# Cluster assignment of an attention and soft-MoE kernel: scores folded by a matmul, one argmax per head pair, and a new order table

## The chip, the cores and the metric

The kernel runs on one core of a Trainium2 chip, as one launch. The metric is the device time of the launch in microseconds (us), lower is better. TensorE (PE in the rows, PEld its weight loads) multiplies, VectorE (DVE), ScalarE (ACT) and GpSimd (POOL) do the elementwise work and the reductions, SyncE (SP) only issues transfers.

## The reference

Three layers in a row, all in fp32. Cut to what matters here:

```python
# 1. attention inside clusters: 2 batches, 8 heads, 768 tokens, 64 dims, 16 centroids per head
q_assign = argmax(q_n @ c_n.T, -1); k_assign = argmax(k_n @ c_n.T, -1)   # rows normalised
scores = where(q_assign[:, None] == k_assign[None, :], q @ k.T / 8, -1e9)
attn = softmax(scores); x = (attn @ v)            # -> 1536 tokens x 512
# 2. soft MoE: 8 experts x 4 slots, hidden 1024
logits = x @ phi; d = softmax(logits, axis=0); slot_in = d.T @ x
slot_out[e] = relu(slot_in[e] @ w1[e]) @ w2[e]; x = softmax(logits, axis=1) @ slot_out
# 3. gated MLP: xn = rms_norm(x) * g; out = (silu(xn @ w_gate) * (xn @ w_val)) @ w_out
```

## The kernel before

**Work of the attention.** The 16 heads are taken in 8 pairs (`prepare(i)`), and each pair in two units (`unit(u)`, u = 0 to 15), which are halves of 384 queries. `prepare` loads k, q, v, splits k and q into a high and a low part (`split_hi`, `split_lo`), transposes them (`trans`, `evac`), and for each half g of 384 tokens finds the cluster: `cluster` multiplies k and q with the centroids (the centroids' high and low parts give two partial scores for each cluster), `cevac` copies the result to the tile cs, `clusterT` transposes it by three matmuls with the identity, `part` adds the two partial scores on DVE, `argmax(0..4)` makes a one-hot row on DVE, `onehot` transposes that by three matmuls, and `oq`, `ok` write it on ACT into the tiles q2 and k2 as extra rows, so that the score matmuls mask by themselves. A unit runs six `s1` steps (two matmuls each) with `s1max` on DVE (a maximum over 768 columns), puts the maxima into q2 by `nmT`, `nrow` and the transfer `mrow`, and then runs `s2` (four matmuls), `exp` on ACT, `acc` (sum of the exponentials) on POOL or DVE, and `av` (product with v), six chunks each. It ends with `osb`, the row sums (`lT`; in unit 15 `sums`), the logits (`lgt`, `lgm`, `lga`; in unit 15 `lgx`) and `oT`, `xrow`.

**PSUM.** `ms` is one bank for all small results (cluster scores, the transposed scores and one-hots, `nmT`, `oT`), `big` three double banks, `av` one bank. A step that allocates `ms` waits until every reader of the last owner is done.

**The layers behind.** On DVE and ACT the attention also carries `decode`, which unpacks the weights of layer 3 (tiles da and wgv). `Tail.middle` does the softmax over tokens and the slots (`SITz`), `experts` streams w1 and w2 from HBM, `gates` forms the small matrices of layer 3 and runs its products (`mm`, `silu`, `hf`, `hh`, `hl`, `om`). `warm` steps are bf16 matmuls of the identity with no use of the result.

**What sets the order.** No engine's program is written by hand. Each step goes to `Sched.op` with a cost per engine and a key (its place in the loop plus an offset by step name from the table `KO`). `Sched.run` takes again and again the step that can start first by these costs, with penalties for steps far ahead of the smallest key, and writes it to its engine. So engines that a step may choose from, and the order on each, come out of the costs, the keys and the constants at the head of the file.

Of the kernel before, what the change touches and what calls it, by code (L numbers as in the profile page):

```python
# [75 lines left out]
LP = 29661.17
AP = 30323.71
GP = 23437.43
XP = 14193.79
# [5 lines left out]
    "argmax": -7.66, "oevac": 15.28, "clusterT": 4.46, "lsum": 18.79, "onehot": -17.16, "acc": -43.2, "av": 64.39,
    "evac": 5.39, "bits": -14.11, "nmT": -27.66, "split_lo": -113.15, "s1max": -11.37, "cevac": -22.81, "nrow": 27.7,
    "cluster": 3.33, "csum": -9.29, "lga": -29.9, "lgm": 53.33, "hh": -53.74, "pre": -21.81, "rms0": -0.9, "h2e": 1.32,
    "part": 19.55, "low": 34.12, "soh": 0.05, "hl": -64.4, "gh": 33.13, "cTe": 9.36, "raw": -14.6, "om": 2.67,
    "cT": -27.78, "sot": -2.04, "lo": 15.35, "gcols": -1.89, "put4": -20.61, "x2s": -1.21, "gp": -3.84, "hi": -13.21,
    "silu": -45.95, "x2": -2.94, "rows": 0.57, "siT": -22.16, "si": -125.5, "dz": 42.07, "mx": 82.62, "mp": 13.33,  # L90
    "dexp": 42.88, "sie": 77.66, "cq": -150.62, "qhi": -37.28, "fexp": 13.02, "gram": -5.42, "socs": 55.02,
    "fold": -5.42, "fsi": -40.68, "fz": 36.93, "qlo": -12.45, "drec": 107.19, "mv": -24.49, "linv": 3.64,
    "xrow": -36.25, "exp": 5.99, "trans": -4.27, "mrow": -111.75, "oq": -72.72, "sums": -65.34, "tok": 8.0,
    "ok": -23.12, "centroids_": 77.19, "cols": 10.87, "csm": -5.47, "ds": -5.05, "dsum": -43.94, "fes": -95.7,
    "four": -35.1, "h1": 30.24, "h2": -10.32, "hT": -3.25, "hTe": -15.51, "hf": -20.81, "high": -60.21, "lgt": -76.92,
    "lgx": -146.73, "lgx0": -3.44, "load": 75.86, "mb": 43.64, "mm": 2.44, "mp1": -72.84, "mpT": 21.92, "od": -23.79,
    "oe": 10.8, "put": 18.97, "relu": -53.54, "rms": 5.79, "root": 18.92, "s2": -1.04, "scale": -12.89, "sel": 28.05,
    "setup": -92.11, "siT0": -14.47, "siTe": -23.07, "side": 117.72, "siz": 10.14, "square": -6.93, "to_out": -29.07,
    "to_tail": 8.19, "to_wp": -25.03, "to_wv": -64.29, "to_wx": 38.05, "to_wz": -23.48, "warm": 89.5, "wload": 21.74,
# [1801 lines left out]
```

## Time and profile before

| | |
|---|---|
| median of 3 runs | 494.79 us (494.28 to 495.96) |
| the profiled execution | 493.6 us, of which 491.9 us from its first to its last instruction |

Stretches of the profiled execution, us from its first instruction:

| stretch | us | PE busy | DVE busy | ACT busy | PE clock | GB/s |
|---|---|---|---|---|---|---|
| to the first s2 of unit 0 | 33.9 | 25.25 | 25.30 | 18.54 | 0.92 | 158 |
| to the first s2 of unit 2 | 26.1 | 25.09 | 18.73 | 17.94 | 0.97 | 128 |
| to the first s2 of unit 14 | 200.5 | 187.79 | 179.94 | 146.81 | 0.99 | 132 |
| to the last logits | 31.7 | 31.12 | 12.88 | 16.49 | 0.94 | 259 |
| middle and experts, to their last product | 56.9 | 52.36 | 10.57 | 12.43 | 0.95 | 374 |
| to the first om of layer 3 | 20.3 | 17.91 | 9.04 | 8.98 | 0.83 | 41 |
| layer 3 | 117.5 | 117.00 | 65.25 | 56.83 | 1.00 | 47 |
| last transfer | 5.0 | 0.05 | 0.00 | 1.17 | 0.77 | 172 |

PE clock is the granted share of 2.4 GHz. A matmul's end is modelled, so that PE busy holds some overlap. A releaser in square brackets (`[0.97 <-DVE E L445]`) is what ended the idle time in front of an instruction.

### The profile page before, as it was taken

The numbers are of one execution on the slowest core, as the hardware profiler recorded it, in microseconds if no ns is written. First come the engines' busy times: TensorE is split into PE (matmuls) and PEld (weight loads), VectorE is DVE, ScalarE is ACT, GpSimd is POOL, SyncE is SP. The second block draws the span as 40 slices with busy tenths as digits, with TensorE's granted clock in tenths as the row PEclk, the third lists the DMA queues.
The fourth block names the chain that finished last, engine by engine and source line by source line (L and its number), as shares of the span: only waits on it lengthen the run. The fifth ranks groups of instructions, "written<-read, shape, count | busy, mean of one in ns | idle before, by whom it ended". The sixth has DMA issues, their size and how long they took to land. (4 is left out here: it accounts for less than half of the span.)

```text
span 491.9 us, 7819 instructions
## 1 busy us (share of the span) xinstructions
PE 456.6 (93%) x2794; PEld 330.3 (67%) x2794; DVE 321.7 (65%) x640; ACT 279.2 (57%) x582; POOL 216.5 (44%) x149
## 2 busy tenths in 40 slices
PE   6889998999999999899889998989989999999995
PEld 5766775777768756667667673335528878888884
DVE  6776889799999899788996143021157894444440
ACT  5568585876877866887756602231066664334332
POOL 2319767674877859484738800012025660000000
PEclk9889998999999999999999978999889999999999
DMA  6455415523634345746236949999502402002002
GB/s 173 117 154 171 115 41 151 135 65 97 198 112 150 94 134 171 200 155 190 98 121 227 339 170 362 378 398 392 225 0 90 168 1 87 0 1 85 0 1 85
DMA packets 30822, 71.96 MB, mean 146 GB/s; under 512 B 4064, under 2 KB 10304, under 8 KB 30784
## 3 DMA queue, kind: packets, MB, share of 16 engines
q1 hardware_dynamic: 26080, 55.73, 34.3%
q10 hardware_dynamic: 4704, 15.73, 10.1%
q8 instruction: 22, 0.36, 0.3%
q14 instruction: 16, 0.13, 0.1%
HBM read 61.97 MB, written 3.15 MB: 132 GB/s over the span
## 5 line engine op out<-in xcount | busy, mean ns | idle before, releaser
L242 POOL TENSOR_TENSOR acc<-acc,P 128x768 f32<-128x768 f32 x62 | 119.3, 1925 | 13.9 <-ACT P L587 10.5
L538 DVE TENSOR_REDUCE nm<-s 128x1 f32<-128x768 f32 x96 | 87.3, 948 | 12.5 <-PE s L526 12.0
L587 ACT ACTIVATE P<-s 128x768 f32<-128x768 f32 x96 | 75.3, 812 | 35.3 <-PE s L580 29.5
L1692 PE MATMUL o<-W,hh 128*128 128x512 f32 x288 | 89.9, 393 | 0.1
L578 PE MATMUL s<-q,k 128*128 128x384 f32 x192 | 70.0, 364 | 2.6 <-DVE nm L538 1.3
L604 PE MATMUL o<-P,rawv 128*64 128x384 f32 x384 | 67.8, 494 | 0.0
L580 PE MATMUL s<-q,k 97*128 97x384 f32 x192 | 65.7, 342 | 0.0
L1692 PEld LDWEIGHTS o<-W,hh 128*128 128x128 f32 x288 | 54.1, 188 | 12.5 <-POOL W L242 0.5
L526 PE MATMUL s<-k,q 96*128 96x384 f32 x192 | 52.4, 369 | 5.3 <-DVE nm L538 4.3
L1692 PE MATMUL o<-W,hl 128*128 128x512 f32 x144 | 56.6, 393 | 0.4 <-DVE hl L242 0.4
L242 POOL TENSOR_TENSOR acc<-P,P 128x768 f32<-128x768 f32 x16 | 30.0, 1875 | 46.3 <-ACT P L587 46.3
L578 PEld LDWEIGHTS s<-q,k 128*128 128x128 f32 x192 | 37.2, 194 | 11.4 <-DVE nm L538 3.4
L604 PEld LDWEIGHTS o<-P,rawv 128*64 128x64 f32 x384 | 25.3, 136 | 28.7 <-issue 27.2
L1664 DVE TENSOR_TENSOR hf<-v,sg 128x512 f32<-128x512 f32 x36 | 24.7, 689 | 28.6 <-ACT sg L1660 27.6
L526 PEld LDWEIGHTS s<-k,q 96*128 96x128 f32 x192 | 31.2, 190 | 16.1 <-DVE nm L538 9.9
L580 PEld LDWEIGHTS s<-q,k 97*128 97x128 f32 x192 | 37.2, 194 | 0.0
L1660 ACT ACTIVATE sg<-g 128x512 f32<-128x512 f32 x36 | 21.4, 597 | 27.7 <-PE g L1652 27.5
L234 ACT CAST hh<-hf 128x512 fp32r<-128x512 f32 x36 | 22.3, 621 | 21.9 <-DVE hf L1664 17.8
L242 DVE TENSOR_TENSOR hl<-hf,hh 128x512 fp32r<-128x512 f32 x29 | 21.2, 731 | 17.0 <-ACT hh L234 16.0
L1692 PEld LDWEIGHTS o<-W,hl 128*128 128x128 f32 x144 | 27.0, 188 | 6.9 <-DVE hl L242 0.8
L242 POOL TENSOR_TENSOR tokk<-rawk,tokk 128x384 fp32r<-128x384 f32 x15 | 16.4, 1092 | 33.3 <-DVE tokk L236 17.6
L676 ACT ACTIVATE pl<-pl 128x128 f32<-128x128 f32 x90 | 23.6, 262 | 7.8 <-PE pl L644 4.0
(261 smaller groups left out, 760.1 us busy)
## 6 DMA issues: line engine op xcount, KB each, us to landing
w<-in_moe_w_dram SPq DMA_DIRECT2D x56, 512.0 KB
gate<-in_moe_w_gate_dram ACTq DMA_DIRECT2D x12, 512.0 KB
val<-in_moe_w_val_dram ACTq DMA_DIRECT2D x12, 512.0 KB
out<-in_moe_w_out_dram SPq DMA_DIRECT2D x10, 512.0 KB
rawk<-in_k_dram SPq DMA_DIRECT2D x8, 384.0 KB
rawq<-in_q_dram SPq DMA_DIRECT2D x8, 384.0 KB
rawv<-in_v_dram SPq DMA_DIRECT2D x8, 384.0 KB
k<-k SPq DMA_DIRECT2D x16, 192.0 KB
```

The lines of the kernel that those rows point to most:

```text
L234: nc.scalar.copy(out, in_)
L242: (nc.vector if e == "dve" else nc.gpsimd).tensor_tensor(out, a, b, op=op)
L526: nc.tensor.matmul(ps[:, g, :HQ], T[q2][0:96, h, qb : qb + 128], T[f"k2_{i}_{g}"][0:96, h, :], start=True, stop=True,)
L538: nc.vector.tensor_reduce(T[f"nm{u}"][:, n : n + 1], T[f"s1_{u}{h}{j}"][:, :, :HQ], op=ALU.max, axis=AX.XY, negate=True)
L578: nc.tensor.matmul(ps[:, h, :HQ], T[f"k1_{i}_{g}"][:, h, kb], T[q1][:, h, :], start=True, stop=False)
L580: nc.tensor.matmul(ps[:, h, :HQ], T[f"k2_{i}_{g}"][0:97, h, kb], T[q2][0:97, h, :], start=False, stop=True)
L587: nc.scalar.activation(p, T[f"s2_{u}_{c}"][:, :, :HQ], AF.Exp, scale=float(1.0 / D**0.5))
L604: nc.tensor.matmul(T[f"o{u}"][64 * h : 64 * h + 64, :HQ], T[f"rawv{i}"][:, h, c, :], T[f"P{u}_{c}"][:, h, :], start=(c == 0), stop=(c == N ...
L676: nc.scalar.activation(p, p, AF.Copy, accum_out=ls_()[:, h, j : j + 1])
L1660: nc.scalar.activation(self.tile(f"sg{tg}_{f}", [128, 512], F32, "sg", "outp", 2), T[f"g{tg}_{f}"], AF.Silu)
L1664: nc.vector.tensor_tensor(self.tile(f"hf{tg}_{f}", [128, 512], F32, "hf", "outp", 2), T[f"v{tg}_{f}"], T[f"sg{tg}_{f}"], op=ALU.mult)
L1692: nc.tensor.matmul(T[f"o{tg}{q}"], T[f"{x}{tg}_{f}"][:, ts], T[f"W{f // 6}"][:, w, f % 6, :], start=(f == 0 and n == 0), stop=(f == 11 and ...
```

## The change

1. **Scores.** Each half still has `cluster` and `cevac`, but cs is now one tile for both halves, in the ring P. `clusterT` multiplies cs by a constant `fold` (128 x 64, made once on DVE), which transposes and adds the two partial scores at once, so `part` is gone.
2. **Argmax.** A new function `both` runs `clusterT`, `argmax`, `onehot`, `oq`, `ok` once per pair for 24 groups of scores, where two halves had 12 each. For pair 0 the work of half 1 no longer has tiles of its own, and one of two `warm` steps goes.
3. **Table.** For pair 0 a one-element exponential follows the two `cevac`, so that ACT loads its exponential table there.
4. **First maxima.** `nmT` of unit 0 uses the bank `av`.
5. **End of the attention.** Unit 15's `sums` write 64 equal columns where they wrote one; the second `sums` comes behind the last `av`, where it was ahead of it; all its `acc` are on DVE.
6. **Behind it.** The row sum of the second softmax (`csm(3)`) waits for the slots; `cols` writes each of its results eight times (64 columns for 8); more `warm` matmuls, eight of them new, ahead of `gram`.
7. **Order.** New constants and a new table `KO`.

```diff
-SH = 6.48
-WM = 0.54
+SH = 2.96
+WM = 2.59
...
-    "oT": -20.92, "s1": -0.82, "lT": 1.82, "split_hi": 67.65, "osb": 5.16, "mag": 19.15, "guard": 7.48,
+    "oT": -33.65, "s1": -0.36, "lT": 2.96, "split_hi": 162.23, "osb": -28.4, "mag": 37.24, "guard": 7.48,
...
-                    nc.tensor.transpose(pt[:, 128 + j * 128 :][:, :128], T[f"cs{i}{g}"][:, at], K["id"])
-
-
-            def part(e):
-                pt = T[f"sc{i}{g}"]
-                for a, b in ((0, 128), (128, 192)):
-                    nc.vector.tensor_reduce(pt[:, a:b].rearrange("p (m c) -> p m c", c=C),
-                                            pt[:, 128 + 2 * a : 128 + 2 * b].rearrange("p (m t c) -> p m c t", t=2, c=C),
-                                            op=ALU.add, axis=AX.X)
...
+                    for j in range(3):
+                        nc.tensor.matmul(T[f"sc{i}"][:, 192 * g + 64 * j :][:, :64], T[f"cs{i}"][:, g, j * 128 : (j + 1) * 128],
+                                         K["fold"], start=True, stop=True)
...
+            p = op({"pe": 700}, clusterT(0), key=zg - 10.25, alloc=("ms",), deps=cv, uses=[CS], after=self.lastE)
...
+                def table(e):
+                    nc.scalar.activation(K["ebias"][64:65, 0:1], K["ebias"][64:65, 0:1], AF.Exp)
...
+        pm = "ms" if u else "av"
...
-                    nc.tensor.matmul(pt[:, 1, HQ + 64 + 2 * n + k : HQ + 65 + 2 * n + k], x, K["ones"], start=True, stop=True)
+                    nc.tensor.matmul(pt[:, k, 64 * n : 64 * n + 64], x, K["ones"].to_broadcast([128, 64]), start=True, stop=True)
...
-            a = op({"act" if k == 2 else "dve": d}, csm(k), deps=[a], key=k0 + 2 + 0.1 * k)
+            a = op({"act" if k == 2 else "dve": d}, csm(k), deps=[a], key=k0 + 2 + 0.1 * k,
+                   after=[self.slots] if k == 3 else ())
...
+            if ep == 3:
+                self.warm(W9, [c], kk + 6.17)
```

**Place one, the first argmax, on DVE.** Pair 0 (scores sc, results am, one-hot E), before:

```order
L412 TENSOR_REDUCE sc_289<-sc_289 128x128
L412 TENSOR_REDUCE sc_289<-sc_289 128x64
...
L436 TENSOR_REDUCE am_303<-sc_289 128x12
L438 TENSOR_TENSOR sc_289<-sc_289,am_303 128x192
L441 SCALAR_TENSOR_TENSOR sc_289<-sc_289,iota 128x192
L443 TENSOR_REDUCE am_303<-sc_289 128x12
L445 TENSOR_TENSOR E<-sc_289,am_303 128x3x2x32
L412 TENSOR_REDUCE sc_314<-sc_314 128x128
```

and now:

```order
L445 TENSOR_REDUCE am_310<-sc_303 128x24
L447 TENSOR_TENSOR sc_303<-sc_303,am_310 128x384
L450 SCALAR_TENSOR_TENSOR sc_303<-sc_303,iota 128x384
L452 TENSOR_REDUCE am_310<-sc_303 128x24
L454 TENSOR_TENSOR E<-sc_303,am_310 128x6x2x32
```

Seven steps for each half (the second half's follow in the same way) became five for the pair. On ACT the four writes of the one-hots for pair 0 stood apart, each half's behind its own one-hot (tiles pe_319 and pe_355), before:

```order
L234 COPY cs_308<-pc_297 128x384
L459 CAST q_0_0_243<-pe_319 32x768
L465 ACTIVATE k_0_0_234<-pe_319,ebias,escale 33x384 x2
L459 CAST q_0_1_277<-pe_355 32x768
L465 ACTIVATE k_0_1_258<-pe_355,ebias,escale 33x384 x2
```

and now:

```order
L236 COPY cs_288<-pc_293 128x384
L495 ACT_TABLE_LOAD
L495 ACTIVATE ebias<-ebias 1x1
L471 CAST q_0_0_246<-pe_318 32x768
L471 CAST q_0_1_279<-pe_318 32x768
L476 ACTIVATE k_0_0_236<-pe_318,ebias,escale 33x384 x2
L476 ACTIVATE k_0_1_260<-pe_318,ebias,escale 33x384 x2
```

They are all behind one one-hot now, and the table load stands ahead of them.

**Place two, the first maxima, on PE.** Names s_0.. are s1 of unit 0, s_1.. of unit 1, pm the maxima of unit 0, sc the scores of pair 1. Before, pm stood behind the scores sc_468 of pair 1's first half in the same bank:

```order
L526 MATMUL s_012_464<-k_0_1_258,q_0_0_243 128x384
L406 MATMUL sc_468<-idr,cs_462 128x128 x3
L358 MATMUL ptq_475<-idr,tokq_1_444 128x128 x6
...
L526 MATMUL s_102_499<-k_0_1_258,q_0_1_277 128x384
L556 MATMUL pm_508<-idr,nm_408 6x128
```

and now, with a bank of its own:

```order
L547 MATMUL s_100_397<-k_0_1_260,q_0_1_279 128x384
...
L547 MATMUL s_012_460<-k_0_1_260,q_0_0_246 128x384
...
L422 MATMUL sc_468<-fold__133,cs_423 128x64 x3
...
L547 MATMUL s_102_472<-k_0_1_260,q_0_1_279 128x384
L580 MATMUL pm_477<-idr,nm_389 6x128
L422 MATMUL sc_468<-fold__133,cs_423 128x64 x3
```

One s1 step of unit 1 (s_100) now stands ahead of the last ones of unit 0.

**Place three, the attention's end, on PE.** Tile o is unit 15's output, pl its sums and logits, before:

```order
L604 MATMUL o_3333<-P_4_3316,rawv_2850 64x384 x2
L661 MATMUL pl_3358<-ones,acc_3281 128x1 x6
L661 MATMUL pl_3358<-ones,P_5_3331 128x1 x6
L681 MATMUL po_3384<-idr,os_3288 128x128 x3
L604 MATMUL o_3333<-P_5_3331,rawv_2850 64x384 x2
L644 MATMUL pl_3358<-phi,os_3392 128x64 x3
```

and now:

```order
L684 MATMUL pl_3227<-ones,acc_3157 128x64 x6
L704 MATMUL po_3245<-idr,os_3166 128x128 x3
L628 MATMUL o_3218<-P_3_3182,rawv_2748 64x384 x2
L628 MATMUL o_3218<-P_4_3190,rawv_2748 64x384 x2
L628 MATMUL o_3218<-P_5_3207,rawv_2748 64x384 x2
L684 MATMUL pl_3227<-ones,P_5_3207 128x64 x6
L668 MATMUL pl_3227<-phi,os_3270 128x64 x3
```

The second group of sums moved behind the last product with v.

## Rows read from the trace of the kernel before

**Rows 1.** The page's slices: granted TensorE clock in 40 equal parts, tenths.

```profile
PEclk9889998999999999999999978999889999999999
```

**Rows 2.** Windows: us, busy PE, PEld, DVE, ACT, POOL (count), clock, DMA share, GB/s.

```profile
60.00:260.50 200.50, 187.79 (x1169) 139.25 (x1169) 179.94 (x339) 146.81 (x333) 136.40 (x79) 0.99 0.45 132
125.50:158.20 32.70, 30.88 (x197) 23.33 (x197) 30.77 (x61) 24.80 (x56) 24.07 (x15) 1.00 0.44 128
```

**Rows 3.** Groups of the whole span, PE: busy us, mean ns, idle before.

```profile
L456 PE MATMUL pe<-idb,E 128*96 128x128 bf16 x48 | 5.8, 231 | 6.1 <-DVE nr L236 4.2 <-DVE E L445 1.6 <-ACT nr L234 0.3
```

**Rows 4.** Groups of the whole span, DVE, same columns.

```profile
L412 DVE TENSOR_REDUCE sc<-sc 128x128 f32<-128x256 f32 x16 | 6.8, 424 | 3.7 <-PE sc L406 2.8 <-ACT pl L676 0.8
L441 DVE SCALAR_TENSOR_TENSOR sc<-sc,iota 128x192 f32<-128x192 f32 x16 | 5.9, 366 | 0.5
...
L436 DVE TENSOR_REDUCE am<-sc 128x12 f32<-128x192 f32 x16 | 5.7, 355 | 0.5
...
L412 DVE TENSOR_REDUCE sc<-sc 128x64 f32<-128x128 f32 x16 | 4.8, 299 | 0.6
...
L1240 DVE TENSOR_REDUCE cs__3554<-Cx 128x12 f32<-128x384 f32 x1 | 0.6, 553 | 0.1
```

**Rows 5.** Timeline of PE in one pair: start us, us, instruction, count.

```profile
134.24 0.49 PE L406 MATMUL sc<-idr,cs 128*128 128x128 f32 x3
134.49 0.42 PE L578 MATMUL s<-q,k 128*128 128x384 f32 x1
...
137.36 0.78 PE L644 MATMUL pl<-phi,os 128*128 128x64 f32 x6
137.98 0.27 PE L556 MATMUL pm<-idr,nm 128*6 128x128 f32 x1
```

**Rows 6.** Timeline of the start, all engines.

```profile
13.17 0.48 ACT L234 COPY cs<-pc 128x384 f32<-128x384 f32 x1 [1.06 <-PE pc L395]
...
17.15 0.36 DVE L445 TENSOR_TENSOR E<-sc,am 128x192 bf16<-128x192 f32 x1
...
18.16 0.79 ACT L459 CAST q<-pe 32x768 fp32r<-32x768 bf16 x1 [0.88 <-PE pe L456]
...
18.96 1.23 ACT L465 ACTIVATE k<-pe,ebias,escale 33x384 fp32r<-33x384 bf16 x2
...
20.99 5.66 DVE L538 TENSOR_REDUCE nm<-s 128x1 f32<-128x768 f32 x6 [2.95 <-PE s L526]
...
29.36 0.27 PE L556 MATMUL pm<-idr,nm 128*6 128x128 f32 x1 [0.97 <-DVE E L445]
...
34.66 1.28 ACT L587 ACT_TABLE_LOAD   x1
```

**Rows 7.** Timeline of the attention's end.

```profile
284.40 1.50 PE L661 MATMUL pl<-ones,acc 128*128 128x1 f32 x12
...
289.13 1.54 PE L644 MATMUL pl<-phi,os 128*128 128x64 f32 x6 [0.57 <-ACT os L234]
...
292.23 6.81 SPq L930 DMA_DIRECT2D w<-in_moe_w_dram  x8
```

**Rows 8.** Windows of 2 us, columns as in rows 2.

```profile
290.00:292.00 2.00, 2.00 (x16) 1.94 (x16) 1.23 (x6) 0.00 (x0) 0.00 (x0) 0.50 0.00 0
304.00:306.00 2.00, 2.00 (x19) 0.44 (x12) 0.00 (x0) 0.00 (x0) 0.00 (x0) 0.69 0.76 279
354.00:356.00 2.00, 2.00 (x12) 1.96 (x12) 0.00 (x0) 0.00 (x0) 0.00 (x0) 0.50 0.03 8
```

**Rows 9.** Timeline of DVE ahead of the experts.

```profile
300.21 0.55 DVE L1240 TENSOR_REDUCE cs__3554<-Cx 128x12 f32<-128x384 f32 x1
...
301.75 0.28 DVE L1213 TENSOR_TENSOR SITz<-siT,rd 128x128 f32<-128x128 f32 x1
```

**Rows 10.** Timeline of PE in the gates.

```profile
353.31 2.74 PE L1448 MATMUL cq<-Q,cc 128*128 128x32 f32 x12
...
355.98 5.69 PE L1538 MATMUL gp<-wgv,SOg 128*64 128x512 f32 x20
```

More of the change, by code (lines that the diff above doesn't have):

```diff
@@ L72 @@
 NF = 12
-PA = 811.82
-LGP = 100.9
+PA = 542.5
+LGP = 15.23
 AVN = 3
[L76 to L79, printed above, removed]
+LP = 29067.49
+AP = 45426.99
+GP = 24760.36
+XP = 1973.86
 NW0, NWX, NWZ, NWV, NW1 = 4, 6, 4, 5, 5
 KO = {
-    "oT": -20.92, "s1": -0.82, "lT": 1.82, "split_hi": 67.65, "osb": 5.16, "mag": 19.15, "guard": 7.48,
[L85 to L99, printed above, removed]
@@ new lines @@
+    "om": 130.13, "cT": -85.64, "sot": -2.04, "lo": 43.2, "gcols": 49.21, "put4": 74.08, "x2s": -1.21, "gp": -71.87,
+    "hi": -2.3, "silu": -59.1, "x2": 17.85, "rows": 0.57, "siT": -32.32, "si": -210.5, "dz": 53.7, "mx": -9.37,
+    "mp": -72.99, "dexp": 70.81, "sie": 78.65, "cq": -130.27, "qhi": -27.84, "fexp": -51.34, "gram": 29.42,
+    "socs": 60.62, "fold": -18.88, "fsi": 19.43, "fz": 17.22, "qlo": -81.51, "drec": 72.66, "mv": -39.92,
+    "linv": -46.1, "xrow": -103.23, "exp": 3.35, "trans": -49.53, "mrow": -68.58, "oq": -165.51, "sums": -125.84,
@@ new lines @@
+    "tok": 8.0, "ok": 5.19, "centroids_": 162.94, "cols": -28.93, "csm": -122.73, "ds": 53.65, "dsum": -95.27,
+    "fes": -64.99, "four": 11.36, "h1": 112.84, "h2": 5.05, "hT": 16.7, "hTe": -74.54, "hf": -7.86, "high": -12.07,
+    "lgt": -57.18, "lgx": -167.12, "lgx0": 40.0, "load": 119.7, "mb": 8.76, "mm": 45.14, "mp1": -12.11, "mpT": 1.18,
+    "od": -61.1, "oe": 14.42, "put": -35.53, "relu": 25.24, "rms": 77.27, "root": 64.03, "s2": -0.0, "scale": -4.33,
+    "sel": 108.81, "setup": -59.12, "siT0": -128.55, "siTe": -76.46, "side": 168.07, "siz": -8.04, "square": -114.39,
@@ L100 @@
+    "table": 31.0, "to_out": -51.93, "to_tail": 39.86, "to_wp": 32.86, "to_wv": -91.74, "to_wx": 30.97,
+    "to_wz": -88.99, "warm": 173.22, "wload": 28.46,
 }
@@ new lines, in half, with both, clusterT, fn @@
+            cv.append(x)
+            rws.append(rows)
+        cv, rws = [], []
+        def both():
+            def clusterT(g):
+                def fn(e):
+                    if g == 0:
+                        self.bank(f"sc{i}")
+                    for j in range(3):
+                        nc.tensor.matmul(T[f"sc{i}"][:, 192 * g + 64 * j :][:, :64], T[f"cs{i}"][:, g, j * 128 : (j + 1) * 128],
+                                         K["fold"], start=True, stop=True)
+                return fn
+            CS = (cv[0], "P")
+            zg = z + DG
+            p = op({"pe": 700}, clusterT(0), key=zg - 10.25, alloc=("ms",), deps=cv, uses=[CS], after=self.lastE)
+            SC = (p, "ms")
+            p = op({"pe": 700}, clusterT(1), key=zg - 10.2, uses=[CS, SC])
@@ L491, in prepare @@
         half(1)
+        both()
         return O
@@ L752, in unit @@
             p = op({"pe": 1340}, sums(0), key=ze - 1, deps=[ac[-1]], alloc=("big",), uses=[ua])
-            pv[-1].after.append(op({"pe": 1340}, sums(1), key=ze - 10, uses=[(ex[-1], "P"), (p, "big")]))
+            last = op({"pe": 1340}, sums(1), key=ze - 10, uses=[(ex[-1], "P"), (p, "big")], after=pv[-1:])
             g = op({"pe": 700}, lgt, key=ze - 10, deps=[self.phi], uses=[(o, "os"), (p, "big")])
@@ L823, in constants @@
     K["mp"] = cpool.tile([128, 32], F32, name="mp0")
+    K["fold"] = early.tile([128, 64], F32, name="fold_")
+    nc.vector.tensor_reduce(K["fold"].rearrange("p (m c) -> p m c", c=C),
+                            K["id"].rearrange("p (m t c) -> p m c t", t=2, c=C), op=ALU.add, axis=AX.X)
     K["escale"] = cpool.tile([128, 2], F32, name="escale")
```

144 lines of the change are left out of this document (75 added, 69 removed).

## The prediction

> **What bounds the kernel now.** I read the page's slices first, then windows cut at the first s2 of units 0, 2 and 14, then the groups by line, then the timeline at the places that the change touches. The clock digits [rows 1] show TensorE at or near its full clock for most of the span, with weak spots at the start, in slices 24 and 25 (283 to 307 us, the attention's end) and in 29 and 30 (344 to 369, the gates). So there are stages with different limits. In the long one, from unit 2 to unit 14, PE is busy 187.79 us of 200.50 and DVE 179.94 [rows 2]: neither is alone the bound. In one head pair of it, 125.50 to 158.20, DVE is busy 30.77 us of 32.70 and PE 30.88. DVE's missing 1.9 us are mostly the small spaces between 61 instructions, so there DVE is full, and PE waits where DVE is late. The group of the one-hot transposes shows it: 6.1 us idle in front of 48 short matmuls, 4.2 of it put down to a small DVE copy, nr, that stands in DVE's queue beside the argmax [rows 3]. The experts' stretch is bound by HBM. Layer 3 is bound by PE, and its matmuls are the same in number, so I count nothing there.
>
> **Scores and argmax, DVE.** The two `part` reductions cost 424 and 299 ns, once per half [rows 4], so 1.45 us per pair go. The five argmax steps lie between 355 and 366 ns each (first and one of the dearest, rows 4), 1.80 us per half and 3.60 per pair. The new ones read 384 columns; the nearest row is a reduction of 384 columns to 12, 553 ns [rows 4], so five cost 2.77. DVE loses 1.45 + 3.60 - 2.77 = 2.28 us per pair, 18 us over eight pairs. Of that only what PE waited for can come back.
>
> **Scores, PE.** Three transposes took 0.25 us of PE's time (134.24 to the next start at 134.49), while three fp32 matmuls with 64 columns, `lgt`, took 0.62 (137.36 to 137.98) [rows 5]. The fold is of the second shape: +0.37 us per half, 0.74 per pair, 5.9 over the kernel, and 4.4 in the twelve halves of the long stretch. PE would then need 187.79 + 4.4 = 192.2 of 200.5 us if its busy time is taken as it stands, so that at most 8.3 us can be gained there, a little more if the modelled ends hide overlap. At the other end, if PE's 12.7 us of idle stay, the stretch grows by 4.4. Since in the pair shown DVE is full and gets 2.28 us of air while PE needs 0.74 more, I take a point nearer the first: **-6 us**. The new table `KO` and the weight on mode switches move steps everywhere in this stretch; I have no row for what an order is worth, so its worth stays in the range.
>
> **Start.** DVE makes `fold` among the constants: a reduction over 128 columns, which I put at 0.3 us by the 299 ns row for the same width [rows 4], on the path. Before, the second half's scores left ACT at 13.65 (13.17 + 0.48), the one-hot was done on DVE at 17.51 and the last `ok` ended at 20.19 [rows 6]. Now scores leave at about 13.95; two folds take 1.24 and a hand-over 0.2, so the argmax starts at 15.4 and ends after 5 x 0.553 and four gaps, at 18.3. Six transposes in place of three add 0.4. Then ACT writes both halves in a row: 2 x 0.79 and twice the 1.23 of a pair of `ok` [rows 6], 4.04 us, where only 2.02 were left before. That ends near 23.4: the first s1 is **3.3 us later**. The six first maxima began at 20.99 and took 5.66 us, to 26.65, yet `nmT` ran at 29.36, released by the argmax of pair 1, which held its bank [rows 6]. The bank `av` takes that wait of 2.7 us away. But one maximum of unit 1 now stands ahead of the last of unit 0, 0.94 us, and a transpose in the `big` ring has to wait for it, so I place the last first maximum at about 32 and `nmT` at 32.3, 2.9 us later than before. The table load of 1.28 us at 34.66 stood in front of the first exponential; it moves to about 14, where ACT waits for the one-hot anyway (if that cover went, it would cost its 1.28). Net: 2.9 - 1.3, and some more because pair 1's argmax comes whole and late: **+2 us** at unit 2, between 0 (the transfer behind `nmT` and PE's in-order s1 steps set the first s2 as before) and +3.3 (nothing is caught up).
>
> The Trainium skill's page "ScalarE: Activation LUTs", in "What ACT_TABLE_LOAD costs", adds a drain of about 1.38 us to a load of 1.28. The trace has the load's 1.28 [rows 6] and no separate drain; by the page the start would cost 1.4 us less than my sum.
>
> **The attention's end.** The first group of sums ran from 284.40 for about 1.4 us, the second as long; then the last `av`, whose result ACT copied while PE idled 0.57, then `lgt` for 1.54 at half clock, and on the last logits waited the transfers that issue from 292.23 on [rows 7]. One column or 64 costs the same per matmul by the two rows (1.50 for 12 records, 0.78 for 6, rows 5 and 7), so the wider sums are free. The second sums now fill the 0.57 of idle, and if the clock stays up `lgt` takes 0.62 in place of 1.54, part of which DVE's steps hide: **-1.1 us** for the restart of the transfers, whose engines stood at 0.00 from 290 to 292 [rows 8]. If the clock falls, -0.5. Unit 15's accumulations on DVE I cost at nothing: DVE is busy 12.88 us of the last 31.7 (the table of stretches). If one were late, it would cost its own length, about that of a maximum over the same 768 columns, 0.94 (5.66 for six, rows 6).
>
> **Middle and experts.** Four steps of the second softmax, from 300.21 on, stand ahead of `SITz` at 301.75 on DVE [rows 9]. With `csm(3)` behind the slots, the experts start 1.5 us sooner. HBM bounds them, so this counts only where transfers ran dry for want of a free buffer: from 304 to 306 the share was 0.76 [rows 8], half a microsecond lost. I take **-0.5**, from 0 to -1.
>
> **Gates.** From 354 to 356 the granted clock was 0.50 [rows 8], in a run of small-column matmuls; `cq` took 2.74 for 12 and the product with the weights 5.69 for 20 [rows 10]. At the full clock `cq` would be 1.4 shorter, and the chain to the first g follows it. The eight new `warm` matmuls stand ahead of `gram`, where PE waits for the copy of its operand, so most of them are hidden; I put 0.2 for the rest. Taken: **-1.5**, from +0.2 to -3.5. `cols` with 64 columns is free by the same rows as the sums.
>
> **Sum.** -6 + 2 - 1.1 - 0.5 - 1.5 = -7.1 us on the profiled execution's 493.6, so 486.5. The median of the runs lies 1.2 above the profiled one, so that the same change gives 494.79 - 7.1; I predict **487.5**.
>
> **Rivals.**
> - *The clock falls all the same* at the attention's end and in the gates. The rows show it at half while PE was busy 2.00 of 2.00 us with small matmuls (rows 8), and nothing about wider ones. Then -6 + 2 - 0.5 - 0.2 + 0.2 = -4.5: 490.3. The skill's page "TensorE: Matmul & The Clock Gate", in "Why this matters for your kernels", names idle gaps between bursts as what brings the slow clock; by it wider columns in a stretch without gaps would change nothing, which is this rival.
> - *PE pays for the fold and does not get its waits back* (slower). If PE's 12.7 us of idle come from its own order and the three `big` banks, DVE's air is of no use: +4.4 in the long stretch and 1.5 elsewhere, +3.3 at the start, -3.1 behind: about 501. It decides once PE's idle in the long stretch falls by less than about 4 us. The full DVE of rows 2 speaks against it; the stretch as a whole, with DVE at 179.94 of 200.50, speaks a little for it.
> - *The gains cancel*: DVE's relief returns just what fold and start cost, 493.5 to 496. Also the case where the change does nothing measurable.
> - *PE's waits vanish and the start is caught up*: -8.3 and what overlap hides, 0 at the start, -3.1 behind: 481 to 483.5.
>
> **Chances.** Forecast 0.50, with its own range 483 to 491.5; clock 0.15; best case 0.12; cancel 0.08; slower 0.15. A difference under 0.3% (1.5 us) can hardly be told from none here. Faster by more: 0.50 + 0.15 + 0.12 = 0.77; same 0.08; slower 0.15. The range leaves out the slower rival and part of the best case: 480.5 to 496.
>
> **What would show it.** Right: the long stretch at some 194 us with DVE near 166 busy and PE's idle at 2 to 4; fold matmuls at 0.6 per half; argmax steps at 0.55; the first s1 near 23.5, `nmT` near 32; the load near 14; transfers that restart about 1 us sooner after unit 15's first products with v, with no dip behind; clock 1.00 at `lgt` and `cq`. Wrong: idle in front of s1 as before, the first s2 of unit 2 more than 4 us late, or new idle on PE behind ACT.

## The result and the profile after

The changed kernel takes 500.74 us (median of 13 runs, 496.88 to 503.90). The kernel before, run beside it, takes 495.5 (13 runs, 494.19 to 498.13). The ratio is 1.010, with a 95% interval of 1.007 to 1.013: slower by about 5 us, where I had forecast 487.5. The profiled execution took 498.6 us, one of the quicker ones, 5.0 more than the 493.6 of before. Below, the ratios leave out a kernel's slow executions, while the times given are medians of all, and the profiled executions of e7, e10 and e14 were slow ones, so nothing is read from their traces.

The page's slices, against [rows 1]:

```profile
PEclk8599999989889899999999999999989999999999
```

The weak slices 24 and 25 at the attention's end and one of the two in the gates are gone. New ones stand in slice 2 (12 to 25 us, digit 5) and in slices 9, 11, 12 and 14 (99 to 174 us), in the middle of the long stretch.

Windows cut at the first s2 of units 2 and 14, and of units 4 and 6, against [rows 2] (us; busy PE, PEld, DVE, ACT, POOL; clock; DMA):

```profile
68.38:271.56 203.18, 190.82 (x1200) 144.68 (x1198) 162.10 (x275) 144.01 (x336) 131.83 (x79) 0.97 0.43 132
98.01:133.31 35.30, 32.77 (x202) 24.76 (x202) 27.58 (x48) 25.12 (x58) 22.96 (x14) 0.94 0.40 118
```

DVE did get its air: 162.10 us busy in place of 179.94, even less than I had counted. But the stretch grew from 200.50 to 203.18, and PE's idle in it is 203.18 - 190.82 = 12.36 us, against 12.71. The air bought nothing. (The +2.7 by itself is no more than two executions of one order differ: e8 below keeps the order of before in this stretch, and took 203.22 in its profiled execution.)

PE's groups over the whole span, against [rows 3]:

```profile
L602 PE MATMUL s<-q,k 128*128 128x384 f32 x192 | 69.5, 362 | 11.4 <-DVE nm L559 10.9 <-ACT P L611 0.4
L422 PE MATMUL sc<-fold__133,cs 128*128 128x64 f32 x96 | 13.5, 284 | 0.0
L465 PE MATMUL pe<-idb,E 128*96 128x128 bf16 x48 | 4.4, 231 | 3.1 <-DVE E L454 3.1
```

The wait for the copy nr in front of the one-hot is gone. In its place PE waits 10.9 us in front of s2 for a maximum (nm). Four waits make 9.9 of it, ending at 98.01, 133.31, 169.82 and 239.61, each at the first s2 of unit 4, 6, 8 or 12. The first of them, rows of DVE and PE:

```profile
92.60 0.96 DVE L559 TENSOR_REDUCE nm<-s 128x1 f32<-128x768 f32 x1 [0.27 <-PE s L547]
93.48 1.39 DVE L991 TENSOR_SCALAR daval<-daval 128x512 int32<-128x512 int32 x1
94.91 2.18 DVE L993 SCALAR_TENSOR_TENSOR wgv<-val,daval 128x512 int32<-128x512 int32 x1
94.94 0.59 PE L547 MATMUL s<-k,q 96*128 96x384 f32 x2
97.01 0.94 DVE L559 TENSOR_REDUCE nm<-s 128x1 f32<-128x768 f32 x1
98.01 0.45 PE L602 MATMUL s<-q,k 128*128 128x384 f32 x1 [2.48 <-DVE nm L559]
```

The maximum that frees PE's bank has its scores at 95.53, but starts at 97.01. Ahead of it in DVE's queue stand two bit steps that unpack a weight of the gates, a stage that comes 250 us later. The granted clock fell to 0.50 for 3.4 us at 98.5, for 6.8 at 132.6 and for 3.4 at 170.2, each within 0.7 us of the end of such a wait; at the fourth wait it did not fall.

The start, against [rows 6] (some rows of three engines):

```profile
14.86 2.65 PE L422 MATMUL sc<-fold__133,cs 128*128 128x64 f32 x12
15.59 1.28 ACT L495 ACT_TABLE_LOAD   x1
17.55 0.56 DVE L445 TENSOR_REDUCE am<-sc 128x24 f32<-128x384 f32 x1 [7.08 <-PE sc L422]
20.01 0.56 DVE L454 TENSOR_TENSOR E<-sc,am 128x384 bf16<-128x384 f32 x1
21.53 1.48 ACT L471 CAST q<-pe 32x768 fp32r<-32x768 bf16 x2 [4.44 <-PE pe L465]
25.00 1.31 PE L547 MATMUL s<-k,q 96*128 96x384 f32 x4
```

The argmax steps are priced right (0.56), and the table load is hidden in ACT's wait, as forecast. But the folds took 2.65 us, at a granted clock of 0.50 that held from 9.8 to 23.4. The first s1 starts at 25.00 instead of 20.37.

The attention's end and the gates, against [rows 7] and [rows 10]:

```profile
296.24 1.55 PE L684 MATMUL pl<-ones,P 128*128 128x64 f32 x12
297.63 0.83 PE L668 MATMUL pl<-phi,os 128*128 128x64 f32 x6
360.14 1.51 PE L1479 MATMUL cq<-Q,cc 128*128 128x32 f32 x12
361.58 3.79 PE L1569 MATMUL gp<-wgv,SOg 128*64 128x512 f32 x20
```

`lgt` takes 0.83 us in place of 1.54, `cq` 1.51 in place of 2.74, the product 3.79 in place of 5.69: the clock stayed up in both places.

The profiled difference by stage: to the first s2 of unit 2 +8.4; from there to unit 14 +2.7; to the last product with v -3.3; to the first h1 -1.3; experts +0.4; gates -1.3; layer 3 and the rest -0.6. Together +5.0. The +8.4 and the -3.3 partly cancel, since the new order does more work ahead of unit 2's s2 (48 matmuls with v up to it, 36 before, and 46 against 42 of s1; PE busy 56.3 us against 50.3, part of it at half clock).

### The profile page after: what moved, and what is told of

Its sections match the earlier page's. It is cut to its first block, busy times and chain, and to the rows that moved or that the text cites. A ratio compares the mean times of both kernels' runs of the same rounds, so it can differ in the third digit from the quotient of the medians.

```text
span 496.9 us, 7891 instructions
## 1 busy us (share of the span) xinstructions
PE 460.2 (93%) x2857; PEld 337.3 (68%) x2857; DVE 305.6 (62%) x562; ACT 276.3 (56%) x593; POOL 205.5 (41%) x146
## 4 chain that ended last, share of the span: by engine, by line
PE 71%; DVE 15%; DMA 8%; issue 2%; ACT 2%; ACTq 0%; POOL 0%; SPq 0%; DVEq 0%; POOLq 0%
PE o L1723 20%; PE o L628 13%; DMA w<-in_moe_w_dram 8%; PE s L602 7%; PE s L604 6%; DVE nm L559 5%; PE s L547 5%; PE pc L397 3%; DVE wgv L993 2%; PE sc L422 2%; PE g L1683 2%; PE v L1683 2%; PE pl L668 1%; PE pl L662 1%; PE po L704 1%
## 5 line engine op out<-in xcount | busy, mean ns | idle before, releaser
L244 POOL TENSOR_TENSOR acc<-acc,P 128x768 f32<-128x768 f32 x60 | 114.4, 1907 | 23.8 <-ACT P L611 18.6
L602 PE MATMUL s<-q,k 128*128 128x384 f32 x192 | 69.5, 362 | 11.4 <-DVE nm L559 10.9
L628 PE MATMUL o<-P,rawv 128*64 128x384 f32 x384 | 70.5, 510 | 0.0
L547 PE MATMUL s<-k,q 96*128 96x384 f32 x192 | 51.3, 367 | 3.1 <-DVE nm L559 1.7
L602 PEld LDWEIGHTS s<-q,k 128*128 128x128 f32 x192 | 36.7, 191 | 22.4 <-DVE nm L559 13.6
L244 POOL TENSOR_TENSOR acc<-P,P 128x768 f32<-128x768 f32 x15 | 27.5, 1831 | 36.4 <-ACT P L611 36.3
L236 ACT COPY os<-o 128x384 f32<-128x384 f32 (+1 forms) x27 | 14.2, 528 | 24.3 <-PE po L704 9.4
```

The costliest lines, as they stand in the source:

```text
L236: nc.scalar.copy(out, in_)
L244: (nc.vector if e == "dve" else nc.gpsimd).tensor_tensor(out, a, b, op=op)
L547: nc.tensor.matmul(ps[:, g, :HQ], T[q2][0:96, h, qb : qb + 128], T[f"k2_{i}_{g}"][0:96, h, :], start=True, stop=True,)
L602: nc.tensor.matmul(ps[:, h, :HQ], T[f"k1_{i}_{g}"][:, h, kb], T[q1][:, h, :], start=True, stop=False)
L628: nc.tensor.matmul(T[f"o{u}"][64 * h : 64 * h + 64, :HQ], T[f"rawv{i}"][:, h, c, :], T[f"P{u}_{c}"][:, h, :], start=(c == 0), stop=(c == N ...
```

## The experiments

"Own order" below means that the recorded sequence of all steps was written into the kernel, so that an edit moves nothing else. Ratios are to the kernel before, each from five rounds, intervals 95%; the changed kernel has 1.010.

**e1_max_first.** Changed kernel, own order, four places on DVE:

```diff
  TENSOR_SCALAR daval<-daval 128x512
+ TENSOR_REDUCE nm<-s 128x1
  SCALAR_TENSOR_TENSOR wgv<-val,daval 128x512
- TENSOR_REDUCE nm<-s 128x1
```

> The changed kernel with its own order kept step by step, but at four places (units 4, 6, 8 and 12) one step on DVE moved: the maximum for which PE's next scores wait goes ahead of the second bit step of a gate weight, not behind it. In the changed kernel's trace that bit step takes 2.18 us there, against 0.68 at its shortest, and PE stands still 2.46 to 2.48 us each time. Theory Q (waits on PE come from single steps that stand ahead in DVE's queue, and the new order set these four): the maximum starts about 1.45 us sooner at each place, 4 x 1.45 = 5.8 us, so 4 to 6 us faster than the changed kernel, a ratio to the kernel before of 0.998 to 1.002. Theory P (PE's own work, the fold above all, is what costs the time): at most 1.5 us faster, a ratio of 1.007 to 1.010.

488.23 us, 0.983 (0.980 to 0.987), twice what theory Q expected. The window of units 2 to 14, and the first of the four places:

```profile
70.12:261.69 191.57, 184.91 (x1199) 141.39 (x1197) 156.40 (x275) 143.55 (x336) 131.85 (x79) 1.00 0.46 140
```

```profile
97.35 0.96 DVE L690 TENSOR_REDUCE nm<-s 128x1 f32<-128x768 f32 x1 [0.71 <-PE s L678]
98.22 0.68 DVE L1124 SCALAR_TENSOR_TENSOR wgv<-val,daval 128x512 int32<-128x512 int32 x1
98.36 0.44 PE L733 MATMUL s<-q,k 128*128 128x384 f32 x1 [1.05 <-DVE nm L690]
```

Each wait fell from 2.48 to 1.05, idle from 12.36 to 6.66: the 5.7 us expected. As much again, 5.9, came from PE's busy time for the same matmuls, with the clock at 1.00 in place of 0.97. Theory P falls: the fold is still there.

**e2_start_clock.** Changed kernel, own order, more warm matmuls:

```diff
-WA0 = 40
+WA0 = 48
+# 8 behind the first and the fourth group of transposes, 24 behind the folds of pair 0
+for n, name in ((8, "wxa"), (8, "wxb"), (24, "wxc")):
+    self.warmx(n, name)
```

> The changed kernel in its own order, with more warm matmuls at the start in PE's idle places: 48 in place of 40 at first, 8 before each of the two score products, 24 behind the folds of pair 0. In the changed kernel's trace the granted clock was 0.50 from 9.8 to 23.4 us, and the folds of pair 0 took 2.65 us for 12 records where 0.78 for 6 was seen later. Theory C (half of the miss at the start is this clock): the clock stays at 1.00, the first scores s1 start at 22.5 to 23.5 instead of 25.0, and the time falls by 1.5 to 2.5 us, a ratio to the kernel before of 1.005 to 1.007. Rival (the chain over DVE's argmax and ACT's copies sets the start whatever the clock): the first s1 stays within 0.7 us of 25.0 and the ratio at 1.009 to 1.011.

496.14 us, 1.0015 (0.9985 to 1.0044). Timeline of the start, and the window in which the changed kernel had 0.50:

```profile
13.29 1.61 PE L553 MATMUL sc<-fold__133,cs 128*128 128x64 f32 x12
...
20.08 2.34 ACT L607 ACTIVATE k<-pe,ebias,escale 33x384 fp32r<-33x384 bf16 x4
...
21.08 0.41 PE L690 MATMUL s<-k,q 96*128 96x384 f32 x1
```

```profile
9.80:23.40 13.60, 10.98 (x119) 9.88 (x119) 6.75 (x13) 9.11 (x15) 2.33 (x3) 1.00 0.52 127
```

Theory C, and more than it asked for: the first s1 at 21.08, only 0.7 later than before, and some 4 us of the whole. The slow start is no accident of one execution. In the traces of e1, e6 and e11, which begin with the changed kernel's steps, the twelve records of the folds took 2.65 to 2.66 us as well, and the first s1 came at 25.89 to 26.71; in e1:

```profile
16.26 2.65 PE L553 MATMUL sc<-fold__133,cs 128*128 128x64 f32 x12
```

The clock column of e1 and e6 reads 1.00 there, but these matmuls are as long as at 0.50 in the changed kernel's trace, so the column is not to be trusted in that place. The four long waits are still in e2 (2.47 us each), and the clock fell at or behind three of them again: at 94.4 for 3.4 us, at 162.7 for 6.8 and at 234.4 for 3.4, not at the second.

**e3_relief_alone** and **e4_fold_alone.** Kernel before, own order; first DVE's relief alone, then PE's side of the fold alone:

```diff
 def part(e):
-    ... two tensor_reduce
+    pass
...
                     elif k == 2:
-                        nc.vector.scalar_tensor_tensor(v, v, 0.0, io, op0=ALU.is_ge, op1=ALU.mult)
+                        pass
```

```diff
-nc.tensor.transpose(pt[:, 128 + j * 128 :][:, :128], T[f"cs{i}{g}"][:, at], K["id"])
+nc.tensor.matmul(pt[:, 192 + j * 64 :][:, :64], T[f"cs{i}{g}"][:, at], K["id"][:, :64], start=True, stop=True)
```

> The kernel before in its own order, with DVE alone relieved: the two part reductions and the third argmax step are left out, so the one-hot rows, and with them the output, are not the reference's. By the rows of before that is 0.424 + 0.299 + 0.366 = 1.09 us per half, 2.18 per pair, 17.4 over the kernel, nearly the relief that the change was counted with; PE's work is as before. Theory D (my prediction: DVE's load is what PE waits for): the long stretch shrinks by 8 to 12 us, a ratio of 0.976 to 0.985. Theory Q (PE waits for single steps and their place in DVE's queue, not for its load): 0 to 3 us, a ratio of 0.994 to 1.000. At the start this also takes about 1 us from the chain to the first s1, which counts within both.

> The kernel before in its own order, with PE's side of the fold alone: in place of the three transposes of a half's scores three matmuls with 64 columns against the first 64 columns of the identity, and the part reductions read those columns twice, so that DVE works as before; the scores, and the output, are not the reference's. Theory P (PE pays its work in full, idle or not): 16 x 0.37 = 5.9 us more, 4.4 of it in the long stretch, a ratio of 1.009 to 1.012. Rival (PE's idle of 12.7 us in that stretch takes most of it up): 0 to 2 us, a ratio of 1.000 to 1.004.

e3: 491.93 us, 0.993 (0.989 to 0.997). e4: 495.1 us, 0.998 (0.995 to 1.001). Windows of units 2 to 14, e3 and then e4:

```profile
58.00:258.58 200.58, 188.82 (x1169) 141.00 (x1169) 168.32 (x304) 146.54 (x333) 137.91 (x80) 0.98 0.45 132
```

```profile
59.92:259.88 199.96, 189.25 (x1202) 142.15 (x1202) 178.05 (x339) 146.45 (x333) 136.60 (x79) 1.00 0.46 132
```

With DVE 11.6 us lighter there, the old order's long stretch stayed at 200.6: PE's idle fell from 12.71 to 11.76 only, and the clock was at 0.50 for 6.8 us in place of 3.4. Theory D falls for the old order, and of the 2.5 us between the two profiled executions 2.0 are at the start. With the fold's matmuls PE's busy time rose by 1.5 us, not 4.4; but the stretch of before holds 3.4 us at 0.50 and e4's none, so by my estimate (half of 3.4) the fold's own work is up to 1.7 more than that. Idle took it up, and the stretch stayed at 200.0.

**e5_both.** The edits of e1 and e2 together.

> The two edits of e1 and e2 together: the maximum ahead of the bit step at four places, and more warm matmuls at the start. e1 ended at a ratio of 0.983 and e2 at 1.0015, the changed kernel at 1.010. If the two losses are separate (theories Q and C): 0.983 less 0.009, a ratio of 0.972 to 0.977, some 484 us. If e1's gain contained the start's (its first s1 was no earlier, 26.71 us, but its clock was): 0.980 to 0.984.

483.12 us, 0.974 (0.972 to 0.977): the two losses are separate and add up. (That e1's clock was full at its start, as I wrote, was a misreading; see e2.)

```profile
63.74:255.22 191.48, 184.84 (x1199) 141.29 (x1198) 156.57 (x275) 143.56 (x336) 131.56 (x79) 1.00 0.47 140
```

**e6_fill_waits.** Changed kernel, own order, the four waits left in and filled:

```diff
+# into the bank "ms", in front of the first s2 of units 4, 6, 8 and 12
+for _ in range(30):
+    nc.tensor.matmul(ps[:, :128], K["idb"], K["idb"], start=True, stop=True)
```

> The changed kernel in its own order with the four waits of 2.46 to 2.48 us left in, but PE given 30 warm matmuls of some 0.073 us in front of each. e1 gained 11.6 us in the long stretch, 5.7 of it idle and 5.9 busy time of PE; in the changed kernel the granted clock was 0.50 for 13.6 us there, and those stretches began at or within 0.5 us of the end of such a wait, or in its course. Theory K (a long wait also brings the slow clock, which costs as much again): with PE kept at work the dips go and the time falls by 4.5 to 6.5 us although the waits stay, a ratio of 0.997 to 1.001. Rival (the dips have another cause, and e1's second half came from the moved step): less than 1.5 us, 1.007 to 1.010.

490.94 us, 0.991 (0.987 to 0.994), better than expected; of the profiled executions 492.95 against 498.6, 5.7 less.

```profile
70.85:268.14 197.29, 191.73 (x1320) 148.11 (x1318) 162.25 (x275) 143.51 (x336) 130.94 (x78) 1.00 0.45 135
```

The stretch is 5.9 us shorter with 120 matmuls more in it. The bit steps ahead of the four maxima are as long as before (1.38 to 1.40 and 2.18 to 2.19 us), so the s2 wait as they did, but with PE at work for all but 0.8 us of each wait; what fell is the slow clock alone. So the clock loss was brought by the waits, and theory K holds.

**e7_nr_first** (and once more for a trace, **e7b_nr_first**). Kernel before, own order; at four places the copy `nr` goes ahead of the bit steps on DVE.

> The kernel before with theory Q's remedy: in its own order, at the four places where PE waits for the copy nr, the bit steps of the gate weights go behind that copy on DVE, not ahead of it. Those waits are 0.87, 0.95, 0.82 and 1.53 us, 4.17 together. Theory Q: 2 to 4 us faster, a ratio of 0.992 to 0.996. Theory D (DVE's load sets the stretch, so that the wait turns up behind the next step): 0.998 to 1.002.

> e7 once more, for a trace: the four waits for nr were taken away and the time did not fall. Theory Q as it now stands (a wait taken away in one place lets the next step on DVE be late): the waits in front of the one-hot fall from 6.1 to some 2.5 us, and those in front of s1 or s2 grow by as much, the idle time of the long stretch staying at 11 to 13 us. Rival: the idle falls by 3 us and more, and the time is lost elsewhere.

498.62 us, 1.002 (0.999 to 1.006): nothing. PE's groups, first the s1 of before, then two of e7b:

```profile
L526 PE MATMUL s<-k,q 96*128 96x384 f32 x192 | 52.4, 369 | 5.3 <-DVE nm L538 4.3 <-ACT q L234 0.5 <-ACT P L587 0.2
```

```profile
L664 PE MATMUL s<-k,q 96*128 96x384 f32 x192 | 54.2, 381 | 7.9 <-DVE nm L676 5.9 <-DVE L L380 1.1 <-ACT q L372 0.5
...
L594 PE MATMUL pe<-idb,E 128*96 128x128 bf16 x48 | 5.8, 232 | 2.9 <-DVE E L583 2.6 <-ACT nr L372 0.3
```

The idle in front of the one-hot fell from 6.1 to 2.9, that in front of s1 rose from 5.3 to 7.9, and PE's idle in units 2 to 14 was 11.8. Here the wait moved: theory Q's remedy does not work everywhere. (e7b took 499.79 us, with the clock at 0.50 for 20.5 us in that stretch, so its time is not read, only its idle.)

**e8_end_only.** Kernel before with the change's edits behind unit 14 (its diff there, nothing else).

> The kernel before with the change's edits behind unit 14 alone: unit 15's accumulations on DVE, the sums of 64 columns and their new place, the second softmax's steps behind the slots, cols of 64 columns, and all warm counts behind the attention; the numbers of the order are those of before, and the order of the attention up to unit 15 is the same. My prediction for these: -1.1 - 0.5 - 1.5 = -3.1 us, a ratio of 0.992 to 0.995. Rival (the clock falls all the same): -0.5 - 0.5 + 0.2, 0.997 to 1.000.

493.36 us, 0.9925 (0.9895 to 0.9956): 3.7 us (2.2 to 5.2), near my 3.1, and the rival is out. Its trace, against that of before, has -1.5 from the first s2 of unit 14 to the last product with v, -1.65 to the first h1, +1.0 in the experts and -1.2 in the gates, -3.3 together. Ahead of that, where the order is that of before, it was slower, with the clock at 0.50 for 10.2 us in units 2 to 14 in place of 3.4:

```profile
61.10:264.32 203.22, 190.81 (x1169) 142.07 (x1169) 179.77 (x339) 147.20 (x333) 138.14 (x81) 0.97 0.44 130
```

**e9_old_numbers** and **e10_new_numbers.** The two halves of the change crossed: new steps with the old KO and constants, old steps with the new ones.

> All of the change but its order: the changed kernel with the numbers of before (the table KO and the constants of the clock model), its warm counts kept. Theory Q (structure good, order bad): no series of long waits on a maximum that comes back in every pair, the end's 3.7 us gained as in e8, some of the argmax's relief too, a ratio of 0.980 to 0.992. Theory P (fold and late argmax cost the time in any order): 1.003 to 1.012. The old numbers were made for another structure, so new waits may come, which the trace would show.

> The order alone: the kernel before with the numbers of the changed kernel, warm counts as before. Theory Q (the new numbers put bit steps ahead of maxima): waits of 2 us and more on a maximum or a one-hot come back pair by pair, the clock falls behind some of them, a ratio of 1.005 to 1.020. Rival (the new numbers suit either structure, and only fold and start are at fault): 0.990 to 1.000.

521.85 us, 1.053 (1.048 to 1.058), and 516.86 us, 1.041 (1.035 to 1.047). Both are far slower than either kernel. These numbers and the structure that they came with belong together; neither cross says which of them is at fault.

**e11_pool_out.** Changed kernel, own order, eight accumulations on POOL left out beside the bit steps in question:

```diff
 def acc(c):
     def fn(e):
+        if (u, c) in OUT:   # (3, 4), (3, 5), (5, 4), (5, 5), (7, 4), (7, 5), (11, 4), (11, 5)
+            return
```

> The changed kernel in its own order, without the eight accumulations on POOL that run beside the bit steps in front of the four waits (the fourth and fifth of units 3, 5, 7 and 11, so that the row sums, and the output, are not the reference's). In the changed kernel's trace the second bit step took 0.67 to 0.69 us in the ten cases before 300 us where POOL was idle at its start, and up to 2.32 in the sixteen where POOL was running. Theory S (the step is stretched while POOL runs): the two steps take about 0.42 and 0.68 at the four places, the waits shrink from 2.48 to about 1.05, the dips behind them go, and the time comes near e1's: a ratio of 0.981 to 0.990. Rival (they are long for another reason): steps and waits as before, 1.005 to 1.010.

487.39 us, 0.982 (0.978 to 0.987). DVE at the first place:

```profile
95.98 0.42 DVE L1127 TENSOR_SCALAR daval<-daval 128x512 int32<-128x512 int32 x1
96.43 0.69 DVE L1129 SCALAR_TENSOR_TENSOR wgv<-val,daval 128x512 int32<-128x512 int32 x1
98.06 0.96 DVE L693 TENSOR_REDUCE nm<-s 128x1 f32<-128x768 f32 x1 [0.94 <-PE s L681]
```

1.39 and 2.18 became 0.42 and 0.69, DVE even waits for PE, and the gain is e1's. Theory S holds. In the kernel before the second step is long too, from 0.67 to 2.32 us; its groups in units 2 to 14 (busy us, mean ns, idle before):

```profile
L966 DVE SCALAR_TENSOR_TENSOR wgv<-val,daval 128x512 int32<-128x512 int32 x12 | 16.3, 1366 | 0.0
L966 DVE SCALAR_TENSOR_TENSOR wgv<-gate,dagate 128x512 int32<-128x512 int32 x11 | 13.9, 1268 | 0.0
```

**e12_fill_cluster.** e5, and at the same places the next half's score product goes ahead of the waiting s2 on PE.

> e5 with one more move at the same four places: the score product of the next half (four matmuls, 0.79 us from first to last in e5's trace) goes ahead of the scores that wait 1.05 us there. Theory Q: 0.6 to 0.8 us at each place, 2.4 to 3.2 together, a ratio of 0.967 to 0.970 where e5 had 0.974. Rival (the next thing, the exponential on ACT or the maxima, then sets the pace): 0.972 to 0.976.

480.38 us, 0.969 (0.965 to 0.974): the fastest of all, 15 us under the kernel before. Against e5 that is some 2.5 us, as expected, though the intervals overlap; the stretch is 2.75 us shorter than e5's.

```profile
63.81:252.54 188.73, 184.92 (x1200) 141.31 (x1198) 156.61 (x275) 143.44 (x336) 131.64 (x79) 1.00 0.46 142
```

**e13_old_order.** All the new steps, each at its place in e8's order.

> All of the change in the order of before, step by step: the changed kernel with each step at the place that it has in e8, the folds and the one argmax of a pair where the second half's stood, a step that is not ready giving way to the next. Against e8 (ratio 0.9925) that leaves fold, one argmax per pair, the av bank and the early table. From e3 (relief alone: 0.993, all of it outside the long stretch) and e4 (fold alone: 0.998) the structure should be worth little where the places of the steps stay: 0.986 to 0.996. Theory D of my prediction (DVE's air comes back to PE, -6 + 2 us more than e8): 0.982 to 0.986. Rival (one late argmax per pair makes new waits on the one-hot, on PE or behind ACT's copies): 0.997 to 1.015.

517.87 us, 1.044 (1.036 to 1.051): outside all three cases, and worse than the last.

```profile
65.67:287.76 222.09, 197.50 (x1208) 145.26 (x1208) 167.23 (x290) 145.84 (x333) 134.41 (x79) 0.97 0.41 119
```

PE idles 24.6 us. Over the whole span 7.0 us of idle stand in front of s2 for the transfer of the maxima (`q<-nr`), 6.4 in front of the one-hot and 3.8 behind ACT's `ok`. The new steps do not fit the places of the old ones.

**e14_load_back** (once more for a trace, **e14b_load_back**) and **e15_load_idle.** e5 with about the saved load put back on DVE, first in the argmax, then where DVE was idle:

```diff
 if k == 0:
-    nc.vector.tensor_reduce(mx, v, op=ALU.max, axis=AX.X)
+    for _ in range(5 if i else 1):
+        nc.vector.tensor_reduce(mx, v, op=ALU.max, axis=AX.X)
```

```diff
+# behind the even unit's logit sums, pairs 1 to 7
+for _ in range(5):
+    nc.vector.tensor_reduce(K["G"], K["id"].rearrange("p (g s) -> p s g", g=4), op=ALU.add, axis=AX.X)
```

> e5 with DVE's relief taken back: in the seven pairs behind pair 0 the first argmax step is done five times over, 4 x 0.55 = 2.2 us more per pair at the place of the argmax, about what fold and single argmax had saved (2.28). e5 had a ratio of 0.974. Theory D' (in the new order DVE's relief is what the gain over before lives on): most of 7 x 2.2 = 15.4 us comes back as waits of PE, 6 to 12 us, a ratio of 0.986 to 0.998. Theory Q (DVE has room there and only places matter): 0 to 3 us, 0.974 to 0.980.

> e14 once more, for a trace: 20 us were lost for 15.4 us of DVE work. Theory Q: the five-fold step holds up the one-hot, and with it the bank that the transposes of the maxima need; so waits of 1.5 us and more in front of these transposes come back in each pair, the granted clock falls behind some of them as in the changed kernel, and both together make the 20 us. Rival: many small waits all over, each time DVE is late.

> e5 with nearly the same extra load on DVE as e14, put elsewhere: in the seven pairs behind pair 0 five idle reductions of 0.375 us, some 1.9 to 2.0 us per pair, 13.5 over the kernel (e14 added 15.4), stand behind the even unit's logit sums, where DVE waited 1.89 us for PE in e5. e14 cost some 20 us. Theory Q (the place decides, not the load): 0 to 3 us, a ratio of 0.974 to 0.980. Theory D' (any load on DVE comes back as waits): 8 to 18 us, 0.990 to 1.010.

e14: 507.83 us, 1.014 (1.009 to 1.019), by the ratios 20 us over e5. e15: 487.25 us, 0.983 (0.977 to 0.988), 4 over e5, a little above theory Q's bound. Groups of e14b:

```profile
L724 PE MATMUL pm<-idr,nm 128*6 128x128 f32 x16 | 4.4, 273 | 12.9 <-DVE E L586 12.3 <-DVE nm L703 0.5
L597 PE MATMUL pe<-idb,E 128*96 128x128 bf16 x48 | 4.0, 220 | 5.9 <-DVE nr L369 4.2 <-DVE E L586 1.8
```

```profile
66.78:274.82 208.04, 187.65 (x1200) 142.44 (x1198) 169.54 (x299) 143.95 (x336) 130.70 (x79) 0.99 0.43 129
```

and the same window of e15:

```profile
65.49:258.38 192.89, 185.39 (x1199) 141.38 (x1197) 164.98 (x300) 143.63 (x336) 131.02 (x78) 1.00 0.45 137
```

The transposes of the maxima (`pm`) share the bank `ms` with the scores, so they wait for the argmax: 12.9 us, where e5 had 0.2. e14b took 502.11 us, with the clock at 0.99; PE's idle in units 2 to 14 is 20.4 against e5's 6.6, which covers 13.8 of the 20 between the two profiled executions. In e15 the stretch holds 8.4 us more of DVE work than e5's and is 1.4 longer. So the argmax is worth its full length at its own place, while of nearly the same work elsewhere 4 us of some 13.5 came back. This is theory D' for the one place, and nearly theory Q for the other.

## Why the prediction was wrong

- **The long stretch, -6, came out at +2.7.** The step that failed is "The new table `KO` and the weight on mode switches move steps everywhere in this stretch; I have no row for what an order is worth, so its worth stays in the range." It was worth more than the whole sum. Four steps in the wrong place in one queue cost some 12 us (e1), and the crosses e9, e10 and e13 cost 20 to 26. The two ends that I did give the stretch were -8.3 and +4.4, and the stated range, 480.5 to 496, left the second one out. (How much of the order comes from `KO` and how much from the new steps stays open.)
- **"DVE is full" was the wrong reading of rows 2.** Part of that busy time was bit steps stretched while POOL ran (shown for the changed kernel by e11). In the stretch of before 23 of them took 30.2 us (the rows at e11), where 0.68 each would be 15.6. With the order held, 11.6 us of relief took 1 us of PE's idle away in that stretch, and nothing of its length (e3). DVE's time counts in full where PE waits behind the very step (e14), and to about a third elsewhere (e15, 4 of 13.5 us).
- **The clock was counted only at the attention's end and in the gates.** In the long stretch the four waits of 9.9 us brought 13.6 us at 0.50, which cost 5.9 more (e6). At the start the clock was at 0.50 for 13.7 us, and the first s1 came 4.6 late. I had +3.3 from the chain; at full clock the chain costs +0.7 (e2): its first s1 starts at 21.08 amid ACT's copies, which end at 22.42, while I had it start behind the last. What brought the clock down at 9.8 is not shown. The argmax in one piece did not: PE's wait of 3.10 us in front of the one-hot begins at 17.5.
- **The end, the middle and the gates were right**: -1.1 - 0.5 - 1.5 forecast, -3.7 measured alone and -1.5 - 0.6 - 1.2 in the trace (e8), with the clock at 1.00 at `lgt` and `cq` in the changed kernel as the first list of signs said. So "the clock falls all the same" is out.
- **The rival at 501 had the time and its sign** (idle fell by 0.35 us, less than 4) **but not the mechanism.** In e1 and e12 the fold is still paid and idle falls to 6.7 and 3.8; alone, the fold cost nothing that could be measured (e4). The time came out by another way, so the match is luck.
- **The sum itself** (494.79 - 7.1 is 487.7, put down as 487.5) was near what the new steps do once four of them stand elsewhere: 488.2 (e1), 483.1 with the start mended (e5). That is not proof of its terms: where in the attention those gains come from, structure or order, cannot be taken apart, since neither half works alone.

## What to carry to other kernels

Before a relieved engine is counted as a gain, find the very instruction behind which the bound engine waits, and ask what the new order puts in front of it; a busy share says little. A long wait of TensorE should be priced twice, once as idle and once as slower matmuls behind it (here 9.9 us and 5.9), and filling it with matmuls of no use already returns the second part. When an order table comes with a structural change, list the few largest waits of the new trace first: moving one step at each may turn the verdict.

## What the hardware showed that I had not expected

A two-input bit step on DVE (`wgv`, and `wo` in two cases, 0.68 us by itself) took 0.67 to 0.69 us in the ten cases of the changed kernel's first 300 us in which POOL was idle at its start. In the sixteen in which POOL was running an accumulation it took 0.70 once and 1.34 to 2.32 otherwise, and without those accumulations 0.69 (e11). The Trainium skill's page "SBUF — State Buffer", in "Who interferes with whom", says that a DVE instruction with two SBUF inputs contends with a GpSimd instruction that reads SBUF, and that issue order decides which of them is blocked. The trace agrees for this step: 0.68 us with POOL idle, up to 2.32 behind an accumulation that was running. The wait shows as busy time of DVE.

Waits of 2.46 to 2.48 us in an otherwise busy PE had a granted clock of 0.50 at or behind them in three cases of four, in the changed kernel and in e2 alike, but not in the same three; with waits of 1.05 at the same places (e1, e5) there was none in the whole stretch. The length of one wait does not decide it: a wait of 1.36 to 1.44 us in front of an s1, ending between 60 and 85 us, had one in seven traces (before, e3, e6, e7b, e8, e11, e15) and none in six (the changed kernel, e1, e2, e5, e12, e14b), and a wait of 2.90 us in e14b, ending at 39.6, had none.
